# Float64 weights turned into float32 in two VectorE steps and a 16-bit ScalarE copy, in an attention and mixture-of-experts kernel

## The chip, the cores and the metric

One core of a Trainium2 chip runs the whole program. The metric is device time in microseconds (us) of one execution. The engines are TensorE (PE; its weight loads are PEld), VectorE (DVE), ScalarE (ACT), GpSimd (POOL) and SyncE (SP), whose queue issues the loads.

## The reference

The program is a chain of three layers over 1536 tokens of width 512.

```
attn: per head and block of 64: out = (q kT * decay) v + (q * powers) state ; state = decay * state + kT v
x  = attn_out reshaped to (1536, 512)
moe:  h = max(x @ w_in, 0) ; x = (h * h) @ w_out            # w_in (512, 2048), w_out (2048, 512)
moe2: logits = x @ w_gate ; each token goes to its best of 8 experts
      out = gate * sigmoid(x @ w_output_gate)[e] * (max(x @ w1[e], 0) @ w2[e])
```

`w_in` and `w_out` are scaled by a numpy float64, so they arrive as float64 (8 bytes a number, 16 MB in all). The kernel has to make float32 of them itself.

## The kernel before

**Attention.** The work is cut into 12 units `u` (two batches, six chunks of 128 tokens each). `emit_T` transposes q and k on PE, and ACT copies the result out (L268, L274). `emit_S` forms the scores, and DVE masks them into `sm` (L295). `emit_O` accumulates the output in the PSUM tile `po`, of which there is one; ACT rounds it into `xTh` (L317), and DVE forms the rest, `xTl` (L318). Only then can PE write `po` for the next unit. `emit_St` updates the state. POOL prepares decayed copies (`qd`, `kd`, `tmp`). In the body of unit u the order is: a weight load, the loads of q and k for u+4 and of v for u+3, `emit_T(u+2)`, `emit_S(u+1)`, `flush()`, `emit_O(u)`, `emit_St(u)`, `wconv`.

**Conversion.** 32 pieces of 128x512 float64 (512 KB each, alternately a block of `w_in` and of `w_out`) are loaded on SP's queue into four staging buffers `st` (`load_w`, L114 and L117). `conv_w` takes a piece's 32-bit halves: ACT scales the upper half into the float32 destination, which puts the exponent right and drops the sign (L131); DVE shifts the lower half right by 29 (L132), joins it with the destination shifted left by 3 (L135), and puts the sign back (L139). The first two are emitted by `wconv`; the last two wait in `rest_` for the next `flush()`. A staging buffer is free for piece i+4 after the last step of piece i. `WL` says how many pieces each unit loads, and `WA` how many it starts to convert.

**First expert layer.** Three chunks of 512 tokens, 16 steps `s` each. `mm1(s)` is 12 matmuls, `mm2(s-2)` 12 more. Every operand is split in a high and a low part (`wih`/`wil`, `woh`/`wol` by `split`, L356 on ACT and L357 on DVE; `gh`/`gl`, L386 and L387). `act1` takes the ReLU (`r`, L376 on ACT) and the square (`g`): in the first chunk on ACT (L379), in the others on DVE (L381). In the first chunk the 16 x 2 weight blocks are also converted and split: each step loads two pieces and converts two until all 32 are done. There is one buffer for `g` and one for `r`.

Each engine runs its instructions in the order of the program. The scheduler of the language adds the waits and moves nothing.

Of the kernel before, what the change touches and what calls it, by code (L numbers as in the profile page):

```python
# [11 lines left out]
BF16 = mybir.dt.bfloat16  # L12
I32 = mybir.dt.int32
I16 = mybir.dt.int16
U32 = mybir.dt.uint32
I64 = mybir.dt.int64
AF = mybir.ActivationFunctionType
ALU = mybir.AluOpType
# [6 lines left out]
def attn_moe_kernel(ctx, tc, q, k, v, lam, w_in, w_out, w_gate, w_ogate, w1, w2, out):  # L25
    nc = tc.nc
# [8 lines left out]
    NF = DFF // P  # L35
# [19 lines left out]
    nc.gpsimd.iota(io8, [[0, 1], [1, E]], base=0, channel_multiplier=0, allow_small_or_imprecise_dtypes=True)  # L55
    slots = const.tile([P, NG * P], I16, name="slots")
    nc.gpsimd.iota(slots, [[1, NG * P]], base=0, channel_multiplier=0, allow_small_or_imprecise_dtypes=True)
# [62 lines left out]
    def conv_w(i):  # L120
        f = i // 2
        t = staged.pop(i)
        if i % 2 == 0:
            dst = wiF[:, :, f * P:(f + 1) * P]
            sh = lambda a: a.rearrange("p (k f) -> p k f", k=KC)
        else:
            dst = woF[:, f, :]
            sh = lambda a: a
        w = t.bitcast(U32).rearrange("p (n w) -> p n w", w=2)
        lo, hi = w[:, :, 0], w[:, :, 1]  # L130
        nc.scalar.activation(out=dst, in_=sh(hi).bitcast(F32), func=AF.Copy, scale=2.0 ** -112)  # L131
        nc.vector.tensor_scalar(out=lo, in0=lo, scalar1=29, scalar2=None, op0=ALU.logical_shift_right)  # L132

        def shifted():
            nc.vector.scalar_tensor_tensor(out=sh(lo), in0=dst.bitcast(U32), scalar=3, in1=sh(lo),  # L135
                                           op0=ALU.logical_shift_left, op1=ALU.bitwise_or)

        def signed():
            nc.vector.scalar_tensor_tensor(out=dst.bitcast(U32), in0=sh(hi), scalar=0x80000000, in1=sh(lo),  # L139
                                           op0=ALU.bitwise_and, op1=ALU.bitwise_or)  # L140
        return shifted, signed


    sa = ExitStack()
# [10 lines left out]
    def cut(shape):  # L155
        n = 1
        for d_ in shape[1:]:
            n *= d_
        i = min(i for i in range(len(cas)) if cuts[i] + n <= KC * F2 // 2)
        o = cuts[i]  # L160
        cuts[i] = o + n
        v_ = cas[i][:, o:o + n]
        if len(shape) == 3:
            v_ = v_.rearrange("p (a b) -> p a b", b=shape[2])
        elif len(shape) == 4:
            v_ = v_.rearrange("p (a b c) -> p a b c", b=shape[2], c=shape[3])
        return v_
# [16 lines left out]
    def load_v(u):  # L184
        b, c = units[u]
        tv = ldv.tile([P, H, D], F32, tag="v", name="v")
        nc.sync.dma_start(out=tv, in_=v[b, :, c * P:(c + 1) * P, :].rearrange("h s d -> s h d"))
        qkv[u].append(tv)
# [56 lines left out]
    for b in range(B):  # L245
        t = cut([P, HP, P])
# [51 lines left out]
    def emit_O(u):  # L298
        b, c = units[u]
        vt = qkv[u][2]  # L300
        sm = sms.pop(u)
        qd = qds.pop(u, None)
        po = pO.tile([P, HP, P], F32, tag="po", name="po")

        if qd is not None:
            for hp in range(HP):
                for a in range(2):
                    sl = slice(a * D, (a + 1) * D)
                    nc.tensor.matmul(out=po[sl, hp, :], lhsT=state[b][:, hp, sl], rhs=qd[:, hp, :], start=hp == 0,  # L309
                                     stop=False)  # L310
        for hp in range(HP):
            for a in range(2):
                h = 2 * hp + a
                nc.tensor.matmul(out=po[a * D:(a + 1) * D, hp, :], lhsT=vt[:, h, :], rhs=sm[:, h, :],  # L314
                                 start=qd is None and hp == 0, stop=hp == HP - 1)
        t0 = b * S + c * P
        nc.scalar.copy(out=xTh[:, :, t0:t0 + P], in_=po)  # L317
        nc.vector.tensor_tensor(out=xTl[:, :, t0:t0 + P], in0=po, in1=xTh[:, :, t0:t0 + P].bitcast(F32),  # L318
                                op=ALU.subtract)

    def emit_tmp(u):
        b, c = units[u]
        if c in (0, NCH - 1):
            return
        tmps[u] = tmp = wa.tile([P, HP, D], F32, tag="tmp", name="tmp")
        for a in range(2):
            sl = slice(a * D, (a + 1) * D)
            nc.gpsimd.tensor_tensor(out=tmp[sl], in0=state[b][sl, :, a * D:(a + 1) * D], in1=lblk[sl], op=ALU.mult)

    def emit_St(u):  # L330
        b, c = units[u]
        vt = qkv.pop(u)[2]
        if c == NCH - 1:
            return
        kd = kds.pop(u)
        pt = pO.tile([P, HP, D], F32, tag="pt", name="pt", bufs=1)
        for hp in range(HP):
            for a in range(2):
                h = 2 * hp + a
                nc.tensor.matmul(out=pt[a * D:(a + 1) * D, hp, :], lhsT=kd[:, h, :], rhs=vt[:, h, :],  # L340
                                 start=True, stop=True)
        tmp = tmps.pop(u, None)
        for a in range(2):
            sl = slice(a * D, (a + 1) * D)
            if c == 0:
                nc.scalar.copy(out=state[b][sl, :, a * D:(a + 1) * D], in_=pt[sl])
                continue
            nc.vector.tensor_add(state[b][sl, :, a * D:(a + 1) * D], pt[sl], tmp[sl])
# [12 lines left out]
    def mm1(s):  # L361
        ch, f = divmod(s, NF)
        wih, wil = wis.pop(s)
        ps = pm.tile([P, NTC], F32, tag="ps", name="ps")
        tk = slice(ch * NTC, (ch + 1) * NTC)
        n = 0
        for kk in range(KC):
            for w_, x_ in ((wih, xTh), (wih, xTl), (wil, xTh)):
                nc.tensor.matmul(out=ps, lhsT=w_[:, kk, :], rhs=x_[:, kk, tk], start=n == 0, stop=n == 3 * KC - 1)  # L369
                n += 1  # L370
        hps[s] = ps

    def act1(s, mid=None):
        ps = hps.pop(s)
        r = gp[0].tile([P, NTC], F32, tag="r", name="r", bufs=1)
        nc.scalar.activation(out=r, in_=ps, func=AF.Relu)  # L376
        g = gp[0].tile([P, NTC], F32, tag="g", name="g", bufs=1)
        if s < NF:
            nc.scalar.activation(out=g, in_=r, func=AF.Square)  # L379
        else:  # L380
            nc.vector.tensor_mul(g, r, ps)  # L381
        if mid is not None:
            mid()
        gh = gp[0].tile([P, NTC], F32R, tag="gh", name="gh")
        gl = gp[0].tile([P, NTC], F32R, tag="gl", name="gl")
        nc.scalar.copy(out=gh, in_=g)  # L386
        nc.vector.tensor_tensor(out=gl, in0=g, in1=gh.bitcast(F32), op=ALU.subtract)  # L387
        gts[s] = gh, gl
# [18 lines left out]
    def wconv(n):  # L407
        m = min(n, NPC - wc[0])
        wc[0] += m
        return [conv_w(wc[0] - m + i) for i in range(m)]  # L410

    rest_ = []

    def flush():
        for step in range(2):
            for r_ in rest_:
                r_[step]()
        rest_.clear()

    WA = (0,0,0,0,1,1,1,1,1,1,2,0)  # L420
    WL = (0,0,1,1,1,1,1,1,1,1,1,1)
    load_v(0)
    load_qk(2)
    load_v(1)
# [8 lines left out]
    for u in range(NU):  # L433

        first = u < 2
        if first:
            emit_O(u)
            emit_St(u)
        emit_tmp(u)
        wload(WL[u])  # L440
        if u + 4 < NU:
            load_qk(u + 4)
        if u + 3 < NU:
            load_v(u + 3)
        if u == 0:
            emit_S(u + 1)
        if first:
            decays(u)
        if u + 2 < NU:
            emit_T(u + 2)  # L450
        if u == NU - 3:

            sqk.close()
            sp[0] = sab.enter_context(tc.tile_pool(name="sp", bufs=2, side="right", reuse_waits="tile"))
        if u == NU - 2:
            split_in(0)
        if 0 < u < NU - 1:
            emit_S(u + 1)
        if u == NU - 2:
            split_in(1)  # L460
        flush()
        if u == NU - 1:
            mm1(0)
        if not first:
            emit_O(u)
            emit_St(u)
        rest_ += wconv(WA[u])
    mm1(1)
    wload(2)
    sa.close()  # L470
# [62 lines left out]
    def route_max(ch):  # L533
        nc.tensor.transpose(p_lg, lgT, ident)
        m8 = const.tile([P, NTT, 8], F32, tag="m8", name="m8")
        i8 = const.tile([P, NTT, 8], U32, tag="i8", name="i8")
        lg = const.tile([P, NTT, 2 * E], F32, tag="lg", name="lg")
# [515 lines left out]
    for e in range(E):  # L1053
        for f in range(NF2):
            s = e * NF2 + f
# [65 lines left out]
```

## Time and profile before

| | us |
|---|---|
| median of 3 runs (561.15 to 562.47) | 562.06 |
| the profiled execution | 560.67 |
| its span, first to last instruction | 558.9 |
| PE busy | 536.4 (96%) |
| DVE busy | 361.6 (65%) |
| ACT busy | 304.1 (54%) |
| granted TensorE clock | 0.995 |

The shares are means over the span. Attention fills the first 68 us, the first chunk of the first expert layer about 68 to 156 us, its other two chunks follow up to about 340 us, and the routed experts take the rest. PE's busy time has gaps in the attention and hardly any in the expert layer.

### The profile page before, as it was taken

Reading aid. Unit: us, or ns where it says so; the run is one execution under the profiler, and the core shown is the slowest. Engines: PE = TensorE matmul, PEld = TensorE weight load, DVE = VectorE, ACT = ScalarE, POOL = GpSimd, SP = SyncE. Lnnn points to the kernel's source line nnn. Section 1 sums busy time; section 2 is a strip of 40 time slices with the busy share of each in tenths; the row PEclk is TensorE's granted clock in tenths of the full one; section 3 lists DMA queues with packets and bytes.
Section 4 is the critical chain, followed back from the end, with each engine's and each line's share of the span. In section 5 each row is a group of like instructions: output and inputs, shape, how many; then the busy total and the mean of one; then the engine's idle time right before and its main releaser. Section 6 shows DMA issues by size and latency. Waiting matters only on the chain.

```text
span 558.9 us, 9785 instructions
## 1 busy us (share of the span) xinstructions
PE 536.4 (96%) x3601; PEld 458.1 (82%) x3601; DVE 361.6 (65%) x728; ACT 304.1 (54%) x580; POOL 149.2 (27%) x149
## 2 busy tenths in 40 slices
PE   7898899999999999999999999999999999999993
PEld 6787788878878888887888888889888889888982
DVE  4789988989455674546676446948264948875610
ACT  4765487776653444445444434447264857884610
POOL 4688000000021232422124241450313142240101
PEclk9999999999999999999999999999999999999998
DMA  8999445568200000000000003999638667830000
GB/s 198 227 245 246 152 153 204 173 205 302 95 1 1 20 34 24 1 0 1 19 20 19 20 0 116 391 228 350 207 114 287 205 206 260 280 133 20 9 24 23
DMA packets 75045, 72.88 MB, mean 130 GB/s; under 512 B 30181, under 2 KB 61029, under 8 KB 74976
## 3 DMA queue, kind: packets, MB, share of 16 engines
q1 hardware_dynamic: 70624, 62.96, 35.9%
q0 software_dynamic: 4064, 8.91, 5.2%
q8 instruction: 43, 0.70, 0.6%
q14 instruction: 26, 0.21, 0.1%
q10 hardware_dynamic: 288, 0.10, 0.1%
HBM read 65.84 MB, written 9.29 MB: 134 GB/s over the span
## 4 chain that ended last, share of the span: by engine, by line
PE 62%; issue 22%; DVE 6%; POOL 4%; DMA 2%; ACT 2%; SPq 1%; POOLq 0%; another core or an unknown queue 0%; ACTq 0%; DVEq 0%
PE acc L497 23%; PE ps L369 22%; PE ph L936 5%; PE ea L958 5%; POOL out_dram L968 3%; POOL xg L895 2%; DMA k<-in_k_dram 2%; PE po L314 1%; PE po L309 1%; PE px L710 1%; PE ps L293 1%; DVE sm L295 1%; DMA out_dram<-y,sidx 1%; DVE xTl L318 1%; PE pl L528 1%
## 5 line engine op out<-in xcount | busy, mean ns | idle before, releaser
L357 POOL TENSOR_TENSOR wol<-woF,woh 128x512 fp32r<-128x512 f32 x32 | 41.3, 1292 | 222.4 <-ACT woh L356 222.4
L387 DVE TENSOR_TENSOR gl<-g,gh 128x512 fp32r<-128x512 f32 x48 | 52.6, 1097 | 65.6 <-ACT gh L386 65.6
L936 PE MATMUL ph<-xh,xTh 128*128 128x192 f32 (+2 forms) x256 | 76.9, 301 | 0.7 <-DVE xl L921 0.4
L369 PE MATMUL ps<-xTh,wih 128*128 128x512 f32 x192 | 76.5, 398 | 0.0
L497 PE MATMUL acc<-gh,woh 128*128 128x512 f32 x192 | 75.0, 390 | 0.5 <-DVE x1T L509 0.5
L497 PE MATMUL acc<-gl,woh 128*128 128x512 f32 x192 | 75.4, 393 | 0.0
L497 PE MATMUL acc<-gh,wol 128*128 128x512 f32 x192 | 74.8, 390 | 0.0
L369 PE MATMUL ps<-xTl,wih 128*128 128x512 f32 x192 | 74.8, 390 | 0.0
L369 PE MATMUL ps<-xTh,wil 128*128 128x512 f32 x192 | 74.8, 389 | 0.0
L936 PE MATMUL ph<-xh,xTl 128*128 128x192 f32 (+2 forms) x256 | 74.7, 292 | 0.0
L951 DVE SCALAR_TENSOR_TENSOR hl<-ph,hh 128x384 fp32r<-128x384 f32 (+1 forms) x64 | 34.2, 534 | 62.1 <-ACT hh L950 49.0
L936 PE MATMUL ph<-xl,xTh 128*128 128x192 f32 (+2 forms) x256 | 74.3, 292 | 0.0
L356 ACT CAST woh<-woF 128x512 fp32r<-128x512 f32 x48 | 29.5, 615 | 57.9 <-PE acc L497 55.7
L936 PEld LDWEIGHTS ph<-xh,xTh 128*128 128x128 f32 x256 | 48.6, 190 | 6.9 <-DVE hl L951 4.3
L950 ACT ACTIVATE hh<-ph 128x384 fp32r<-128x384 f32 (+1 forms) x64 | 30.8, 482 | 37.4 <-PE ph L936 33.3
L936 PEld LDWEIGHTS ph<-xl,xTh 128*128 128x128 f32 x256 | 48.6, 190 | 0.8
L936 PEld LDWEIGHTS ph<-xh,xTl 128*128 128x128 f32 x256 | 48.8, 190 | 0.2 <-DVE xTl L811 0.2
L376 ACT ACTIVATE r<-ps 128x512 f32<-128x512 f32 x48 | 28.5, 594 | 35.5 <-PE ps L369 35.4
L895 POOL DMA_INDIRECT xg<-x1d,gidx x21 | 24.5, 1168 | 83.9 <-PE pt L915 62.3
L968 POOL DMA_INDIRECT out_dram<-y,sidx x23 | 23.7, 1029 | 76.6 <-ACT y L967 73.6
L811 DVE TENSOR_TENSOR xTl<-w1r,xTh 128x512 fp32r<-128x512 f32 x64 | 43.6, 685 | 0.1
L497 PEld LDWEIGHTS acc<-gl,woh 128*128 128x128 f32 x192 | 36.0, 188 | 9.0 <-DVE gl L387 1.6
(189 smaller groups left out, 1154.0 us busy)
## 6 DMA issues: line engine op xcount, KB each, us to landing
w1r<-in_moe_w_dram SPq DMA_DIRECT2D x32, 512.0 KB
w2r<-in_moe_w_dram SPq DMA_DIRECT2D x32, 512.0 KB
st<-in_moe_w_in_dram SPq DMA_DIRECT2D x16, 512.0 KB
st<-in_moe_w_out_dram SPq DMA_DIRECT2D x16, 512.0 KB
q<-in_q_dram SPq DMA_DIRECT2D x24, 128.0 KB
k<-in_k_dram SPq DMA_DIRECT2D x12, 256.0 KB
v<-in_v_dram SPq DMA_DIRECT2D x12, 256.0 KB
x1d<-xr SPq DMA_DIRECT2D x12, 256.0 KB
```

The lines of the kernel that those rows point to most:

```text
L356: nc.scalar.copy(out=hi, in_=src)
L357: eng.tensor_tensor(out=lo, in0=src, in1=hi.bitcast(F32), op=ALU.subtract)
L369: nc.tensor.matmul(out=ps, lhsT=w_[:, kk, :], rhs=x_[:, kk, tk], start=n == 0, stop=n == 3 * KC - 1)
L376: nc.scalar.activation(out=r, in_=ps, func=AF.Relu)
L387: nc.vector.tensor_tensor(out=gl, in0=g, in1=gh.bitcast(F32), op=ALU.subtract)
L497: nc.tensor.matmul(out=acc[ch][cb], lhsT=w_[:, cs], rhs=x_, start=f == 0 and i == 0, stop=f == NF - 1 and i == 2)
L811: eng.tensor_tensor(out=lo, in0=src, in1=hi.bitcast(F32), op=ALU.subtract)
L895: nc.gpsimd.indirect_dma_start(out=out_, out_offset=None, in_=x1d[:, :], in_offset=bass.IndirectOffsetOnAxis(ap=ix, axis=0), bounds_check= ...
L936: nc.tensor.matmul(out=ps[:, 0:N], lhsT=w_[:, kk, :], rhs=x_[:, kk, 0:N], start=n == 0, stop=n == 3 * KC - 1)
L950: nc.scalar.activation(out=hh[:, f, ts_], in_=ps[:, ts_], func=AF.Relu)
L951: nc.vector.scalar_tensor_tensor(out=hl[:, f, ts_], in0=ps[:, ts_], scalar=0.0, in1=hh[:, f, ts_].bitcast(F32), op0=ALU.max, op1=ALU.subtract)
L968: nc.gpsimd.indirect_dma_start(out=outs[j][:, :], out_offset=bass.IndirectOffsetOnAxis(ap=sidx[:, j, e:e + 1], axis=0), in_=ys[j], in_offs ...
```

## The change

A piece's lowest three mantissa bits, which lie at the top of the lower half, are first brought next to the upper half's bits: ACT copies 16 bits of the lower half over the low 16 bits of the upper half (after the scaled copy has read it). One DVE instruction then shifts the upper half right by 13, with its sign, and masks it to the sign and three bits. A second one joins that with the destination shifted left by 3. So DVE runs two instructions for each piece instead of three, and ACT two instead of one; and DVE's first one now comes after ACT's copy. `flush()` has one step, and runs once more behind the attention's last unit. The square of the first chunk is taken on DVE, as in the other chunks. By `WL` the attention loads pieces from unit 3 on instead of 2, nine instead of ten; by `WA` it starts to convert them in unit 5 instead of 4, seven instead of eight.

```diff
+        h = t.bitcast(U16).rearrange("p (n w) -> p n w", w=4)
         nc.scalar.activation(out=dst, in_=sh(hi).bitcast(F32), func=AF.Copy, scale=2.0 ** -112)
-        nc.vector.tensor_scalar(out=lo, in0=lo, scalar1=29, scalar2=None, op0=ALU.logical_shift_right)
-
-        def shifted():
-            nc.vector.scalar_tensor_tensor(out=sh(lo), in0=dst.bitcast(U32), scalar=3, in1=sh(lo),
+
+        nc.scalar.copy(out=h[:, :, 2], in_=h[:, :, 1])
+        nc.vector.tensor_scalar(out=lo.bitcast(I32), in0=hi.bitcast(I32), scalar1=13, scalar2=-0x7ffffff9,
+                                op0=ALU.arith_shift_right, op1=ALU.bitwise_and)
+
+        def join():
+            nc.vector.scalar_tensor_tensor(out=dst.bitcast(U32), in0=dst.bitcast(U32), scalar=3, in1=sh(lo),
                                            op0=ALU.logical_shift_left, op1=ALU.bitwise_or)
-
-        def signed():
-            nc.vector.scalar_tensor_tensor(out=dst.bitcast(U32), in0=sh(hi), scalar=0x80000000, in1=sh(lo),
-                                           op0=ALU.bitwise_and, op1=ALU.bitwise_or)
-        return shifted, signed
+        return join
...
-        if s < NF:
-            nc.scalar.activation(out=g, in_=r, func=AF.Square)
-        else:
-            nc.vector.tensor_mul(g, r, ps)
+        nc.vector.tensor_mul(g, r, ps)
...
-        for step in range(2):
-            for r_ in rest_:
-                r_[step]()
+        for r_ in rest_:
+            r_()
...
-    WA = (0,0,0,0,1,1,1,1,1,1,2,0)
-    WL = (0,0,1,1,1,1,1,1,1,1,1,1)
+    WA = (0,0,0,0,0,1,1,1,1,1,1,1)
+    WL = (0,0,0,1,1,1,1,1,1,1,1,1)
...
         rest_ += wconv(WA[u])
+    flush()
     mm1(1)
```

In the changed kernel's line numbers the loads stand one higher, `conv_w` one to four higher, the rest up to the square one higher, and what follows the square two lower. SP's queue in units 1 to 3, before: `st` is a staging buffer.

```order
L179 DMA q<-in_q_dram 64x4x128 x2
L181 DMA k<-in_k_dram 128x8x64
L187 DMA v<-in_v_dram 128x8x64
L114 DMA st<-in_moe_w_in_dram 128x4x128
L179 DMA q<-in_q_dram 64x4x128 x2
L181 DMA k<-in_k_dram 128x8x64
L187 DMA v<-in_v_dram 128x8x64
L117 DMA st<-in_moe_w_out_dram 128x512
```

The same place of the change:

```order
L180 DMA q<-in_q_dram 64x4x128 x2
L182 DMA k<-in_k_dram 128x8x64
L188 DMA v<-in_v_dram 128x8x64
L180 DMA q<-in_q_dram 64x4x128 x2
L182 DMA k<-in_k_dram 128x8x64
L188 DMA v<-in_v_dram 128x8x64
L115 DMA st<-in_moe_w_in_dram 128x4x128
```

The first piece has moved behind the q, k and v of one more unit, and every later piece with it. So five pieces instead of six stand ahead of the last k.

VectorE at the end of the attention, from the scores of the last unit to the low part of step 2's weights, before:

```order
L295 TENSOR_TENSOR sm<-ps,ca_142 128x4x128 x2
L357 TENSOR_TENSOR wil<-wiF,wih 128x512
L135 SCALAR_TENSOR_TENSOR st<-woF,st 128x512
L139 SCALAR_TENSOR_TENSOR woF<-st 128x512
L318 TENSOR_TENSOR xTl<-po,xTh 128x4x128
L132 TENSOR_SCALAR st<-st 128x512 x2
L135 SCALAR_TENSOR_TENSOR st<-wiF,st 128x512
L135 SCALAR_TENSOR_TENSOR st<-woF,st 128x512
L139 SCALAR_TENSOR_TENSOR wiF<-st 128x4x128
L139 SCALAR_TENSOR_TENSOR woF<-st 128x512
L318 TENSOR_TENSOR xTl<-po,xTh 128x4x128
L357 TENSOR_TENSOR wil<-wiF,wih 128x512
```

And in the change:

```order
L296 TENSOR_TENSOR sm<-ps,ca_142 128x4x128 x2
L358 TENSOR_TENSOR wil<-wiF,wih 128x512
L140 SCALAR_TENSOR_TENSOR wiF<-wiF,st 128x4x128
L319 TENSOR_TENSOR xTl<-po,xTh 128x4x128
L136 TENSOR_SCALAR st<-st 128x512
L140 SCALAR_TENSOR_TENSOR woF<-woF,st 128x512
L319 TENSOR_TENSOR xTl<-po,xTh 128x4x128
L136 TENSOR_SCALAR st<-st 128x512
L140 SCALAR_TENSOR_TENSOR wiF<-wiF,st 128x4x128
L379 TENSOR_TENSOR g<-r,ps 128x512
L358 TENSOR_TENSOR wil<-wiF,wih 128x512
```

One instruction instead of two stands ahead of the first `xTl` here, and two instead of six between the two. But a shift, a join and the square now stand between the last `xTl` and `wil`, where nothing stood.

ScalarE in one step of the first chunk, from the ReLU to the last conversion, before:

```order
L376 ACTIVATE r<-ps 128x512
L379 ACTIVATE g<-r 128x512
L356 CAST woh<-woF 128x512
L356 CAST wih<-wiF 128x512
L386 CAST gh<-g 128x512
L131 ACTIVATE wiF<-st 128x4x128
L131 ACTIVATE woF<-st 128x512
```

And in the change:

```order
L377 ACTIVATE r<-ps 128x512
L357 CAST woh<-woF 128x512
L357 CAST wih<-wiF 128x512
L384 CAST gh<-g 128x512
L133 ACTIVATE woF<-st 128x512
L135 COPY st<-st 128x512
L133 ACTIVATE wiF<-st 128x4x128
L135 COPY st<-st 128x512
```

The square is gone, and each scaled copy is followed by a 16-bit copy; the pieces of a step are now `w_out` first, then `w_in`, since an odd number is converted ahead.

## Rows read from the trace of the kernel before

**Rows 1.** The page: rate of transfers in 40 slices, and packets.
```profile
GB/s 198 227 245 246 152 153 204 173 205 302 95 1 1 20 34 24 1 0 1 19 20 19 20 0 116 391 228 350 207 114 287 205 206 260 280 133 20 9 24 23
DMA packets 75045, 72.88 MB, mean 130 GB/s; under 512 B 30181, under 2 KB 61029, under 8 KB 74976
```

**Rows 2.** Busy time of three stretches: each engine, clock, DMA share, GB/s.
```profile
34.00:55.00 21.00, 17.20 (x316) 15.37 (x316) 20.48 (x31) 13.21 (x28) 18.20 (x18) 1.00 0.97 247
55.00:69.00 14.00, 12.17 (x167) 10.58 (x164) 13.74 (x26) 6.71 (x14) 2.13 (x2) 1.00 0.55 167
101.00:142.00 41.00, 41.00 (x179) 32.67 (x178) 35.58 (x66) 28.76 (x51) 0.00 (x0) 1.00 0.71 246
```

**Rows 3.** TensorE in order of time, 53 to 72 us: start, duration, idle time before.
```profile
54.78 0.46 PE L263 MATMUL psT<-ident,k 64*128 64x64 f32 x8 [0.91 <-DMA k<-in_k_dram]
...
60.69 1.09 PE L309 MATMUL po<-qd,ca 128*64 128x128 f32 x16 [1.05 <-DVE xTl L318]
...
66.38 1.09 PE L309 MATMUL po<-qd,ca 128*64 128x128 f32 x16 [0.78 <-DVE xTl L318]
...
68.28 0.50 PE L369 MATMUL ps<-xTh,wih 128*128 128x512 f32 x1
...
71.49 0.19 PEld L369 LDWEIGHTS ps<-xTh,wil 128*128 128x128 f32 x1 [0.15 <-DVE wil L357]
```

**Rows 4.** SyncE's queue, issues of q: first and last of two stretches.
```profile
5.53 2.35 SPq L179 DMA_DIRECT2D q<-in_q_dram  x2
...
16.75 1.69 SPq L179 DMA_DIRECT2D q<-in_q_dram  x2
...
21.25 1.26 SPq L179 DMA_DIRECT2D q<-in_q_dram  x2
...
48.65 1.26 SPq L179 DMA_DIRECT2D q<-in_q_dram  x2
```

**Rows 5.** The chain that ended last: the last k, and the first chunk.
```profile
50.03 4.71 DMA k<-in_k_dram
...
101.26 2.79 PE acc L497 x12
104.04 2.72 PE ps L369 x12
...
142.94 2.27 PE ps L369 x10
```

**Rows 6.** VectorE in order of time, 59 to 66 us.
```profile
59.25 0.69 DVE L139 SCALAR_TENSOR_TENSOR wiF<-st 128x512 uint32<-128x512 uint32 x1
59.86 0.68 DVE L318 TENSOR_TENSOR xTl<-po,xTh 128x512 fp32r<-128x512 f32 x1
...
64.94 0.69 DVE L139 SCALAR_TENSOR_TENSOR woF<-st 128x512 uint32<-128x512 uint32 x1
65.55 0.68 DVE L318 TENSOR_TENSOR xTl<-po,xTh 128x512 fp32r<-128x512 f32 x1
```

**Rows 7.** Groups by form on VectorE and ScalarE: busy us, mean ns, idle before.
```profile
L132 DVE TENSOR_SCALAR st<-st 128x512 uint32<-128x512 uint32 x32 | 12.6, 430 | 0.2
...
L381 DVE TENSOR_TENSOR g<-r,ps 128x512 f32<-128x512 f32 x32 | 21.9, 684 | 11.7 <-ACT r L376 11.7
...
L131 ACT ACTIVATE wiF<-st 128x512 f32<-128x512 f32 x16 | 11.0, 686 | 1.8 <-DMA st<-in_moe_w_in_dram 1.4
```

**Rows 8.** Waits in 99 to 146 us: total, times, longest.
```profile
ACT g L379 <- DVE gl L387: 8.8, 9, 2.9
```

**Rows 9.** ScalarE and VectorE in order of time at the first chunk's start.
```profile
68.39 0.59 ACT L317 CAST xTh<-po 128x512 fp32r<-128x512 f32 x1 [3.98 <-PE po L314]
...
69.57 0.63 ACT L379 ACTIVATE g<-r 128x512 f32<-128x512 f32 x1
70.11 0.60 ACT L356 CAST wih<-wiF 128x512 fp32r<-128x512 f32 x1
...
70.74 0.69 DVE L357 TENSOR_TENSOR wil<-wiF,wih 128x512 fp32r<-128x512 f32 x1 [0.82 <-ACT wih L356]
```

More of the change, by code (lines that the diff above doesn't have):

```diff
@@ L14 @@
 I16 = mybir.dt.int16
+U16 = mybir.dt.uint16
 U32 = mybir.dt.uint32
```

## The prediction

> **What bounds the kernel now.** I read the busy time by stretches first, then TensorE's own idle time, and then what ended it. From 101 to 142 us PE is busy for 41.00 of 41 us [rows 2], and the expert layers behind that look alike: what is gained ahead of them is kept, what is lost ahead of them is paid. The gaps are in the attention. From 34 to 69 us PE is busy for 29.4 of 35 us, while DVE is busy for 34.2 of them and the DMA engines, up to 55 us, at 0.97 of their time [rows 2]. So two things are full at once there, and the order of time tells which of them ends PE's waits. At 54.78 us PE waits 0.91 us for the last k [rows 3], which was issued at 50.03 and took 4.71 us to come [rows 5]. That is a queue in front of the DMA engines, and the chain runs through it. Behind it the chain is DVE: at 60.69 and 66.38 us PE waits 1.05 and 0.78 us for `xTl` [rows 3], that is for the single `po` to be free. Each time `xTl` stands right behind conversion steps [rows 6]. The first chunk shows a third thing. Its blocks take 2.72 us where nothing is missing [rows 5], but from 101.26 to the start of the `mm1` block at 142.94 us there are 15 blocks in 41.68 us, where 15 x 2.72 is 40.80: 0.88 us are lost. DVE is busy for 35.58 of 41 us there and its idle time is forced: ACT's square waits for `gl` [rows 8], since there is one `g`, and the split behind it on DVE waits for ACT in turn.
>
> **The loads.** One piece fewer stands ahead of the last k on SP's queue. SP issues q, k and v of three units in 11.22 us without pieces (5.53 to 16.75), 3.74 each, and of five units with one piece each in 27.40 us (21.25 to 48.65), 5.48 each [rows 4]. The piece costs the difference, 1.74 us. The bounds: by bytes at the stretch's 247 GB/s [rows 2], 512 KB take 2.12 us; at the highest rate of any slice, 391 GB/s [rows 1], 1.34 us. I take 1.75, since it is measured on this queue: **-1.75**.
>
> The Trainium skill (DMA: Bandwidth & Descriptors, Specifications) says that transfers under 512 bytes don't reach the line rate, and gives a ceiling of 435 GB/s. 30,181 of the packets here are under 512 bytes [rows 1]; the rows of k and v are 256 bytes, those of the pieces 1 and 4 KB. By its ceiling a piece would take 1.2 us, an estimate, and the sum below would be 3.0 us and not 3.56. That the piece costs less than its bytes at the mean rate agrees; by how much is what the queue's rows say.
>
> Does the rest keep pace? DVE loses one join of the two in every unit, at 0.69 us and above [rows 6], and the whole first conversion, so it no longer fills its time. The first conversion's loads and steps keep their distance of two units.
>
> **The end of the attention.** Ahead of each of the two late `xTl` one instruction of 0.69 us goes [rows 6], and DVE comes to them earlier, because it lags less. With one join, the first `xTl` needs only `xTh` (0.59 us on ACT [rows 9]) and itself (0.68), 1.3 us behind the end of `emit_O`; on PE `emit_St` and `emit_S` lie behind that for about 1.6 us. The second has all of `mm1(0)` as its cover, 2.72 us, against masks, a split and a join on DVE that start earlier by the first wait. So both waits go: **-1.83**. The bound is what one join of 0.69 us at each would give, 1.38, less a little for the new wait of the shift on ACT's 16-bit copy: 1.2.
>
> **The 16-bit copy.** The trace has none. From below, ACT's cast of as many elements takes 0.60 us [rows 9]; the scaled copy, which also reads every second word, 0.686 [rows 7]. I take 0.69, since it has the same stride. Twice that, 1.4 us, would be writing at half the rate. In the attention it stands where ACT waits for PE (3.98 us before the last `xTh` [rows 9]). In the first chunk a step of ACT then holds four instructions of 0.60 and four of 0.69 us, 5.2 us, against 5.44 for two blocks of PE, and successive ones overlap a little (0.63 us of square, 0.54 from its start to the next [rows 9]). It fits, narrowly. If that cover is gone, each 0.1 us of the copy costs 0.2 us a step.
>
> **The new shift** has one tensor operand as the old one, 0.43 us [rows 7]. If two operations made it as slow as a join, 0.69, DVE would still have room. In order, it holds the masks and splits behind it until ACT's copy is done; ACT's copy comes right behind `xTh`, and the shift behind two state additions, so I price it at nothing, except here:
>
> **The start of the first chunk** pays. Before, ACT ran `xTh`, `r`, `g`, `wih`, and DVE's `wil` started 2.35 us after `xTh` did (68.39 to 70.74 [rows 9]); PE, which needs it for its third matmul of `mm1(2)`, waited 0.15 us [rows 3]. Now the last piece's two copies come between `xTh` and `r`, and DVE has shift, join and square ahead of `wil`. In start-to-start times: `xTh` 0.5, two copies 1.2, the shift 0.4, the join 0.6, `g` 0.6, which makes 3.3 us. `wil` starts 0.95 us later, and PE's wait grows by about as much: **+0.9**. The bounds are 0.5, if joins and copies overlap better, and 1.2, with full durations. What is late next is `gl` of step 1, by the same amount; it has about 1 us to spare before `mm2(1)`.
>
> **The first chunk** then runs as DVE and PE let it. DVE's step was two shifts, two splits, four joins and `gl`; now two joins are gone and the square (0.684 [rows 7]) is added: 2 x 0.43 + 6 x 0.69 = 5.0 us, and by start-to-start times 4.4. More important, `g` no longer crosses from `gl` to ACT and back. Both engines are under 5.44, so the 0.88 us come back: **-0.88**; from below, 0.4, if ACT is late now and then. There is one step more with a conversion, and the first experts' loads follow one step later (about 5 us), some 200 us before they are used: nothing.
>
> **The sum.** -1.75 - 1.83 + 0.9 - 0.88 = -3.56. The profiled execution took 560.67 us, 558.9 of them in its span; it would take 557.1. The median of the runs is 562.06, so I forecast **558.5 us**. With all bounds at their good end the gain is 2.12 + 1.83 + 0.88 - 0.5 = 4.3, at their bad end 1.34 + 1.2 + 0.4 - 1.2 = 1.7: 557.7 to 560.3.
>
> **Rivals.**
> - *The loads don't hurry the attention.* DVE has no idle time there, so the k may be late by chance of the same rhythm, or the queue may lose the time elsewhere, as q, k and v of later units wait for buffers that POOL frees (busy for 18.2 of 21 us [rows 2]). Against it: PE does wait for k, with the whole queue filled. Then 1.75 fall away: 560.3 us. Chance 0.13.
> - *The start and the handshake eat it.* DVE's shift waits for ACT in each unit and step, ACT for DVE's `g` before `gh`. If the start of the first chunk costs 3.5 us more instead of 0.9, as three waits of a join and a copy in a row would, it is 561 to 562.5 us: no change. For it: ACT has 0.25 us to spare in a step by full durations. Against it: the waits of a step don't close a circle. Chance 0.09.
> - *ACT becomes the bound of the first chunk.* With a copy of 1.4 us its step is 4 x 0.54 + 2 x 0.6 + 2 x 1.3 = 6.0 us, 0.55 over PE's, in 12 steps 6.6, less about 1 us of slack, and the 0.88 are not won: 562.06 - 2.7 + 5.6 = 565 us. It begins at about 1.05 us for a copy and makes the kernel slower from about 1.3. For it, nothing but that a 16-bit write isn't in the trace; against it, that ACT's other forms lie between 0.59 and 0.69. Chance 0.08.
>
> **The numbers.** The forecast with its bounds has 0.70. A change under 0.2%, 1.1 us, is about what cannot be told from none. Faster is the forecast and the first rival, 0.83; same is the second, 0.09; slower the third, 0.08. For 8 in 10 I take the forecast and the first rival with 0.7 us at the low end for the unknown and 0.6 at the high end: 557.0 to 560.9.
>
> **What would show it.** In the changed profile the last k should land near 53 us, and no wait for `xTl` of over 0.3 us should stand behind it; `mm1(1)` should start near 64.8 us instead of 68.28. PE's third matmul of `mm1(2)` should wait about 1 us for `wil`. From 100 to 140 us the blocks should be 2.72 us each, with ACT busy for about 5 us a step. The 16-bit copy should take 0.6 to 0.75 us, the shift 0.43. I am wrong if the copy takes over 1 us, if k lands at 54.7 us again, or if PE waits for `gl` or for `r` in the first steps.

## The result and the profile after

The changed kernel takes 565.12 us (median of 8 runs, 564.14 to 566.88) against 561.61 us (8 runs) before, on the same chip: a ratio of 1.0073, 95% interval 1.0056 to 1.0091. It is slower by 3.5 us where 3.6 us less were forecast, and it lies outside the range. The third rival came about: ScalarE becomes the bound of the first chunk. The profiled execution took 566.84 us, the second longest of the eight and 1.7 over their median; 565.1 of them lie in its span, 6.2 over the one of before. So the split by stages below is that of a dear execution.

Busy time of the stretches of [rows 2], in the changed kernel (TensorE, weight loads, VectorE, ScalarE, GpSimd, clock, DMA share, GB/s):

```profile
34.00:55.00 21.00, 17.98 (x332) 16.54 (x332) 17.77 (x30) 18.73 (x34) 17.48 (x18) 0.96 0.99 253
55.00:69.00 14.00, 13.38 (x157) 11.49 (x156) 9.26 (x16) 8.98 (x15) 1.42 (x1) 0.93 0.45 133
...
101.00:142.00 41.00, 40.64 (x171) 31.29 (x170) 31.64 (x57) 40.56 (x58) 0.00 (x0) 1.00 0.59 183
```

In the attention VectorE falls from 20.48 to 17.77 of 21 us, as the change means it to. From 101 to 142 us ScalarE goes from 28.76 to 40.56 of 41 us: it has no idle time left. TensorE still shows 40.64, but it starts 171 matmuls there instead of 179. A busy time close to full is no proof of full speed; the count beside it is what tells.

ScalarE in order of time, one step of the first chunk (start, duration):

```profile
100.05 0.71 ACT L377 ACTIVATE r<-ps 128x512 f32<-128x512 f32 x1
100.64 0.62 ACT L357 CAST woh<-woF 128x512 fp32r<-128x512 f32 x1
101.14 0.64 ACT L357 CAST wih<-wiF 128x512 fp32r<-128x512 f32 x1
101.66 0.64 ACT L384 CAST gh<-g 128x512 fp32r<-128x512 f32 x1
102.18 0.69 ACT L133 ACTIVATE woF<-st 128x512 f32<-128x512 f32 x1
102.90 1.39 ACT L135 COPY st<-st 128x512 uint16<-128x512 uint16 x1
104.01 0.72 ACT L133 ACTIVATE wiF<-st 128x512 f32<-128x512 f32 x1
104.76 1.38 ACT L135 COPY st<-st 128x512 uint16<-128x512 uint16 x1
105.86 0.70 ACT L377 ACTIVATE r<-ps 128x512 f32<-128x512 f32 x1
```

No row waits. From `r` to the next `r` there are 5.81 us, and two blocks of TensorE are 5.44. The two copies hold 1.11 and 1.10 of it from start to start, the scaled copies ahead of them 0.72 and 0.75.

The groups of the copy, the shift and the square in the first 156 us (busy us, mean ns, idle before), beside [rows 7]:

```profile
L135 ACT COPY st<-st 128x512 uint16<-128x512 uint16 x32 | 44.1, 1379 | 1.0
L136 DVE TENSOR_SCALAR st<-st 128x512 int32<-128x512 int32 x32 | 14.2, 443 | 20.0 <-ACT st L135 19.9
L379 DVE TENSOR_TENSOR g<-r,ps 128x512 f32<-128x512 f32 x16 | 11.0, 687 | 1.1 <-ACT r L377 1.0
```

The shift (0.443 us) and the square (0.687) cost what was said; the copy takes 1.379 us instead of 0.69. The waits from 69 to 157 us (total, times, longest) show what has taken the place of the wait in [rows 8]:

```profile
DVE st L136 <- ACT st L135: 18.9, 15, 1.4
PEld ps L370 <- DVE wil L358: 5.6, 12, 0.6
PE ps L370 <- DVE g L379: 2.4, 2, 1.6
```

VectorE no longer holds ScalarE up; it waits for ScalarE's copy in every step, and TensorE's weight loads, twelve times, for the split `wil` behind it.

TensorE in order of time, from the last k to `mm1(2)`, beside [rows 3]:

```profile
53.53 0.69 PE L264 MATMUL psT<-ident,k 64*128 64x64 f32 x8 [1.64 <-DMA k<-in_k_dram]
54.01 2.02 PE L294 MATMUL ps<-ca 64*128 64x128 f32 x16
55.97 1.52 PE L310 MATMUL po<-qd,ca 128*64 128x128 f32 x16
...
59.86 1.09 PE L310 MATMUL po<-qd,ca 128*64 128x128 f32 x16
...
65.40 1.09 PE L310 MATMUL po<-qd,ca 128*64 128x128 f32 x16 [0.62 <-DVE xTl L319]
...
67.30 0.50 PE L370 MATMUL ps<-xTh,wih 128*128 128x512 f32 x1
...
71.91 0.47 PE L370 MATMUL ps<-xTh,wih 128*128 128x512 f32 x1 [1.58 <-DVE g L379]
...
74.82 0.39 PE L495 MATMUL acc<-gh,woh 128*128 128x512 f32 x1
```

The last k lands 1.25 us earlier, the first wait for `xTl` is gone, and `mm1(1)` starts at 67.30 instead of 68.28. Then `mm1(2)` waits 1.58 us, and for `g`, not for `wil`. Comparing marks in the two traces splits the 6.2 us: up to `mm1(1)` -0.98; to the first matmul of `mm2(0)` (73.89 before, 74.82 after) +1.91; to the last `gl` of the chunk (160.24 before, 165.96 after) +4.79; behind it +0.5.

The chain of waits now leads through the copy. By engine (ScalarE had 2% before), and two of its links:

```profile
PE 66%; ACT 14%; issue 10%; DVE 4%; DMA 2%; POOL 1%; POOLq 0%; SPq 0%; another core or an unknown queue 0%; ACTq 0%
```

```profile
102.90 1.39 ACT st L135
...
104.76 1.38 ACT st L135
```

### The profile page after: what moved, and what is told of

Same layout as the page of the kernel before. It is cut to its first block, busy times and chain, and to the rows that moved or that the text cites. A ratio compares the mean times of both kernels' runs of the same rounds, so it can differ in the third digit from the quotient of the medians.

```text
span 565.1 us, 9816 instructions
## 1 busy us (share of the span) xinstructions
PE 542.5 (96%) x3601; PEld 460.5 (81%) x3601; DVE 351.8 (62%) x712; ACT 332.8 (59%) x596; POOL 146.7 (26%) x149
## 4 chain that ended last, share of the span: by engine, by line
PE 66%; ACT 14%; issue 10%; DVE 4%; DMA 2%; POOL 1%; POOLq 0%; SPq 0%; another core or an unknown queue 0%; ACTq 0%
PE acc L495 18%; PE ps L370 16%; PE ph L934 13%; PE ea L956 11%; ACT st L135 6%; ACT gh L384 1%; PE ps L294 1%; ACT woF L133 1%; ACT wiF L133 1%; PE po L310 1%; ACT ca L269 1%; PE po L315 1%; DMA k<-in_k_dram 1%; PE px L708 1%; PE pt L913 1%
## 5 line engine op out<-in xcount | busy, mean ns | idle before, releaser
L370 PE MATMUL ps<-xTh,wil 128*128 128x512 f32 x192 | 76.2, 397 | 0.7 <-DVE wil L358 0.2
L377 ACT ACTIVATE r<-ps 128x512 f32<-128x512 f32 x48 | 30.2, 630 | 37.0 <-PE ps L370 37.0
L370 PEld LDWEIGHTS ps<-xTh,wil 128*128 128x128 f32 x192 | 36.0, 188 | 13.0 <-DVE wil L358 5.6
L370 PEld LDWEIGHTS ps<-xTh,wih 128*128 128x128 f32 x192 | 36.1, 188 | 11.1 <-ACT wih L357 2.6
L135 ACT COPY st<-st 128x512 uint16<-128x512 uint16 x32 | 44.1, 1379 | 1.0
```

The source lines that it names most:

```text
L135: nc.scalar.copy(out=h[:, :, 2], in_=h[:, :, 1])
```

## The experiments

**Theory A:** the copy costs twice what was assumed, and this alone makes ScalarE the bound of the first chunk; the other terms hold. **Theory B:** the new handshakes (shift for copy, `gh` for `g`) make the steps longer, whatever the copy takes. With them goes the question why the copy takes so long. Each ratio is to runs of the kernel before on the same chip.

**The copy at the price of a word.** ScalarE copies a whole 32-bit word at the same place, over the lower half, and VectorE's shift still comes after it; the lowest three bits of the mantissa are then other bits.

```
-        nc.scalar.copy(out=h[:, :, 2], in_=h[:, :, 1])
+        nc.scalar.copy(out=lo.bitcast(F32), in_=hi.bitcast(F32))
```

> The changed kernel with its 16-bit copy replaced by a copy of 32-bit words of the same pieces, at the same place and with the same waits (the three lowest mantissa bits of the weights are then other bits). Theory A, the price of the 16-bit copy (1.38 us in the changed profile) makes ScalarE the bound of the first chunk: the copy should take about 0.69 us, ScalarE's step fall from 5.80 to about 4.5 us of starts, TensorE's from 5.80 to 5.44, and the time to 557.5 to 559.5 us, under before's 561.6. Theory B, the waits of VectorE's shift and square on ScalarE cost the time whatever a copy takes: 562 us or more.

Measured: 557.96 us, ratio 0.9934 [0.9910, 0.9958], span 555.5 where the sum of the prediction gave 555.3. The copy's group, TensorE's marks, and links of the chain:

```profile
L135 ACT COPY st<-st 128x512 f32<-128x512 f32 x32 | 20.9, 654 | 0.0
```

```profile
52.63 0.46 PE L264 MATMUL psT<-ident,k 64*128 64x64 f32 x8 [0.63 <-DMA k<-in_k_dram]
...
57.82 1.09 PE L310 MATMUL po<-qd,ca 128*64 128x128 f32 x16 [0.32 <-DVE xTl L319]
...
64.68 0.50 PE L370 MATMUL ps<-xTh,wih 128*128 128x512 f32 x1
...
68.44 0.47 PE L370 MATMUL ps<-xTh,wih 128*128 128x512 f32 x1 [0.72 <-DVE g L379]
...
71.34 0.39 PE L495 MATMUL acc<-gh,woh 128*128 128x512 f32 x1
```

```profile
101.43 2.72 PE ps L370 x12
104.15 2.72 PE acc L495 x12
```

With a copy of 0.654 us the sum lands, and with it `mm1(1)` at 64.68 (forecast 64.8) and the blocks of 2.72. The handshakes are all still there, but the shift waits for ScalarE for only 2.4 us in all in the first chunk, against 18.9, so B falls.

**What in the copy is dear.** A kernel of copies alone (all else of the computation is left out), 128x512 each, four of each form, on tiles of 8-byte groups.

```
+        nc.scalar.copy(out=dense(ts["readstr_o"]), in_=low(ts["readstr_i"]))
+        nc.scalar.copy(out=high(ts["writestr_o"]), in_=dense(ts["writestr_i"]))
```

> A probe that leaves out the whole computation and runs copies of 128 x 512 elements, four of each form: 16 bits in place with a step of 8 bytes as in the change (1.38 us is known), the same into another tile, dense to dense, step to dense, dense to step, the same bits as bfloat16, and 32-bit words with a step and dense; then the form of the change on VectorE and on GpSimd. If the 16-bit write with a step is what costs, dense to step is about 1.38 us and step to dense about 0.6. If the read is, the reverse. If the integer type is, the bfloat16 form is about 0.65 and dense to dense of 16-bit integers stays high. If reading and writing the same tile is, the form into another tile is about 0.65.

The groups (busy us, mean ns):

```profile
L55 ACT COPY inplace<-inplace 128x512 uint16<-128x512 uint16 x4 | 5.6, 1409 | 0.0
...
L57 ACT COPY dense_o<-dense_i 128x512 uint16<-128x512 uint16 x4 | 3.1, 780 | 0.0
L58 ACT COPY readstr_o<-readstr_i 128x512 uint16<-128x512 uint16 x4 | 2.9, 720 | 0.0
L59 ACT COPY writestr_o<-writestr_i 128x512 uint16<-128x512 uint16 x4 | 5.4, 1358 | 0.0
L60 ACT COPY bfl<-bfl 128x512 bf16<-128x512 bf16 x4 | 5.4, 1359 | 0.0
L61 ACT COPY word<-word 128x512 f32<-128x512 f32 x4 | 2.9, 728 | 0.0
```

Reading 16 bits every 8 bytes is cheap (0.720), writing them there is dear (1.358); another type (bf16, 1.359) or another tile (1.450) changes nothing, and a 32-bit word at the same step is cheap in both directions (0.728). So it is the write of half words with a step, on this engine: VectorE's first copy of the same form took 0.67 us. Why ScalarE takes so long for it no run shows.

**The old three steps with the square on VectorE and the later loads.** (The conversion of before, rest of the change.)

```
-        nc.scalar.copy(out=h[:, :, 2], in_=h[:, :, 1])
...
+        nc.vector.tensor_scalar(out=lo, in0=lo, scalar1=29, scalar2=None, op0=ALU.logical_shift_right)
...
+        return shifted, signed
```

> The three-step conversion of before with the rest of the change (loads and conversions one unit later, one flush more, square of the first chunk on VectorE). Theory A: no 16-bit copy, so the first chunk isn't bound by ScalarE; VectorE's step is 2 x 0.38 + 8 x 0.60 = 5.6 us of starts, about before's 5.57; the attention gains from the loads: 559.5 to 561.5 us. Theory B (moving the square to VectorE makes the start and the steps wait): 563 us or more.

Measured: 560.15 us, 0.9970 [0.9956, 0.9985]. VectorE is busy for 41.00 of 41 us from 101 to 142 us, and the blocks still take 2.72; waits for `xTl` of 0.94 and 0.76 us stay.

**The later loads alone** (the kernel before, with the new `WA`, `WL` and the last `flush`).

```
+    WA = (0,0,0,0,0,1,1,1,1,1,1,1)
+    WL = (0,0,0,1,1,1,1,1,1,1,1,1)
```

> Before with the new numbers of loads and conversions per unit alone (and the flush that they need). If the loads are worth what the forecast said, the last k lands about 1.75 us earlier; VectorE still has two joins in each unit, so part of it may stay at VectorE: 559.5 to 561 us. If VectorE alone set the attention's length: 561 to 562 us, no change.

Measured: 560.20 us, 0.9972 [0.9957, 0.9987]. TensorE no longer waits for the last k; `mm1(1)` starts at 66.59 instead of 68.28, and the waits for `xTl` are 0.65, 0.94 and 0.78 us. The loads, with the conversions one unit later, are worth about 1.4 us by themselves. They also bring a cost at the start of the first chunk: a piece now stands between the last unit's output and `mm1(2)`, whose weight loads wait for both splits behind it:

```profile
69.63 0.19 PEld L369 LDWEIGHTS ps<-xTh,wih 128*128 128x128 f32 x1 [0.44 <-ACT wih L356]
...
70.53 0.19 PEld L369 LDWEIGHTS ps<-xTh,wil 128*128 128x128 f32 x1 [0.60 <-DVE wil L357]
```

This kernel and the one above differ only in the engine that takes the square in the first chunk, and their times agree. The marks show why. From `mm1(1)` to `mm2(0)` there are 6.34 us (66.59 to 72.93) with ScalarE's square and 6.91 (67.42 to 74.33) with VectorE's, against 5.61 before; from there to the last `gl` of the chunk 86.19 (to 159.12) and 85.47 (to 159.80), against 86.35 before. What the square's move wins in the steps it loses, but for 0.15 us, at the start.

**The new conversion alone**, with ScalarE's square and the old loads.

```
+        if s < NF:
+            nc.scalar.activation(out=g, in_=r, func=AF.Square)
+        else:
+            nc.vector.tensor_mul(g, r, ps)
```

> Before with the new conversion alone (square on ScalarE, loads and conversions per unit as before). Theory A: ScalarE's step is 5.80 plus a square of 0.54, 6.3 us of starts, 0.77 over before's 5.57 in 12 steps, 9 us, and the attention has one copy more: 568 to 573 us. If moving the square was a loss by itself, this is faster than the change: under 565.

Measured: 571.34 us, 1.0194 [1.0170, 1.0219]. From 101 to 142 us ScalarE is busy for 40.40 us and TensorE for 38.12; a step takes 6.48 us. One more instruction on ScalarE costs 0.67 us a step: ScalarE is the bound, as A has it.

**Half of the pieces.** Only those of `w_in` get the 16-bit copy, those of `w_out` the old three steps.

```
+        if i % 2 == 0:
...
+            nc.scalar.copy(out=h[:, :, 2], in_=h[:, :, 1])
```

> The change with only the w_in pieces converted with the 16-bit copy, the w_out pieces in the three steps of before. Theory A: ScalarE's step is 4 x 0.53 + 2 x 0.70 + 1.10 = 4.6 us, VectorE's 2 x 0.38 + 7 x 0.60 = 5.0 us, both under TensorE's 5.44: the first chunk runs without loss, 558 to 560 us. Theory B: 562 us or more.

Measured: 559.36 us, 0.9965 [0.9949, 0.9981]. One copy of 1.38 us a step fits: from 85 to 150 us all blocks but two (2.96 and 2.75) take 2.72 us.

**The first chunk's copies on GpSimd.**

```
-        nc.scalar.copy(out=h[:, :, 2], in_=h[:, :, 1])
+        (nc.scalar.copy if i < 7 else nc.gpsimd.tensor_copy)(out=h[:, :, 2], in_=h[:, :, 1])
```

> The change with the first chunk's 16-bit copies on GpSimd, which is idle there, and the attention's seven left on ScalarE. Theory A: ScalarE's step falls to 4 x 0.53 + 2 x 0.60 = 3.3 us, the first chunk runs at 5.44 a step if GpSimd's copy takes under about 2.2 us, and the time is 559 to 561.5 us; if GpSimd's copies hold up VectorE's instructions of two SBUF operands, 561.5 to 564. Theory B, the waits of VectorE on another engine's copy: 563 us or more.

Measured: 566.80 us, 1.0118 [1.0103, 1.0134], over both ranges of theory A. It lies in the range of B, but not by B's waits: from 69 to 155 us VectorE's shift waits for GpSimd's copy for 1.3 us in all. GpSimd's copy takes 1.632 us; GpSimd, two copies in one row, and VectorE in order of time beside it:

```profile
99.66 3.13 POOL L135 COPY st<-st 128x512 uint16<-128x512 uint16 x2 [2.97 <-ACT woF L133]
...
99.39 0.67 DVE L140 SCALAR_TENSOR_TENSOR woF<-woF,st 128x512 uint32<-128x512 uint32 x1
99.99 1.58 DVE L140 SCALAR_TENSOR_TENSOR wiF<-wiF,st 128x512 uint32<-128x512 uint32 x1
101.49 1.59 DVE L385 TENSOR_TENSOR gl<-g,gh 128x512 fp32r<-128x512 f32 x1
```

The same join takes 0.67 or 1.58 us, and VectorE is busy for 41.00 of 41 us from 101 to 142 us. The Trainium skill (SBUF — State Buffer, "SBUF: two separate sides") says that a VectorE operation with two SBUF inputs and a GpSimd operation that reads SBUF exclude each other for a whole instruction. The trace agrees: beside GpSimd's copies a join and `gl` are each stretched by 0.9 us in every step. The traces of before and of the change held the sign already, in `gl` from the end of the first chunk on, where GpSimd makes the splits `wol`: 1.37 and 1.36 us instead of 0.69.

**A wide write.** ScalarE reads the half word and writes a 32-bit word; VectorE keeps both joins and loses the shift.

```
+        nc.scalar.activation(out=lo, in_=h[:, :, 1], func=AF.Copy, scale=2.0 ** -13, bias=-4095.5 / 8192)
```

> The change with another second ScalarE instruction: it reads the same 16 bits with a step, scales them by 2 to the -13 and writes the three bits as a 32-bit word into the lower half, so VectorE needs no shift and runs the two joins of before. By the copy forms, a read of 16 bits with a step and a wide write should take about 0.7 us. Theory A (the 16-bit write with a step is the cost): ScalarE's step is 4 x 0.53 + 4 x 0.60 = 4.5 us, VectorE's 8 x 0.60 = 4.8 us, both under 5.44: the first chunk without loss; the attention as in the run with the loads alone: 558.5 to 560 us. If the read of 16 bits with a step costs too, 563 us or more.

Measured: 559.75 us, 0.9968 [0.9950, 0.9986]. The group shows a half word read and a word written at 0.675 us:

```profile
L134 ACT ACTIVATE st<-st 128x512 uint32<-128x512 uint16 x32 | 21.6, 675 | 0.0
```

The joins remain, and so do waits for `xTl`, 1.05 and 0.44 us.

**The joins behind `xTl`.** The same, with `flush()` behind `emit_O` and `emit_St` instead of ahead of them; and the old three steps with the same move.

```
-        flush()
         if u == NU - 1:
             mm1(0)
         if not first:
             emit_O(u)
             emit_St(u)
+        flush()
```

> The same with the joins of each unit behind that unit's output instead of ahead of it on VectorE, so that the low part of the output doesn't wait for them. If the two late waits of TensorE for it (0.94 and 0.78 us in the run with the loads alone) stem from the joins ahead of it, they go: 1 to 1.7 us less than the run with the wide write, 557 to 558.5 us. If the work is only moved to the next unit's masks, the same as that run.

> The three-step conversion of before with the rest of the change (560.2 us) and the joins behind each unit's output. If the late waits go as above: 558.5 to 559.5 us; if they are only moved, 560 us.

Measured: 560.20 us, 0.9979 [0.9967, 0.9991], and 562.40 us, 1.0012 [0.9994, 1.0030]. The gain came in neither: the first can't be told from the run with the wide write (559.75), which is the second of the two outcomes expected, and the other is slower than both that were expected. The late waits for `xTl` are gone in both, and come back behind them. TensorE in the first of the two:

```profile
65.52 0.50 PE L371 MATMUL ps<-xTh,wih 128*128 128x512 f32 x1
...
70.34 0.47 PE L371 MATMUL ps<-xTh,wih 128*128 128x512 f32 x1 [1.78 <-DVE g L380]
```

In the second `mm1(2)` waits 2.35 us for `g`, and ahead of that TensorE waits for the last masks and then runs its scores slowly (granted clock 0.65 from 58 to 61 us):

```profile
58.29 2.51 PE L293 MATMUL ps<-ca,ca 64*128 64x128 f32 x16 [1.55 <-DVE sm L295]
```

What VectorE doesn't do ahead of `xTl` it does ahead of the masks and of the square of step 0.

**New conversion where ScalarE has room, old one where not.** Pieces 0 to 5 (the attention's, but for its seventh) the new way, the other 26 the old way; in the first of two kernels the square of step 0 is on ScalarE again.

```
-        if i % 2 == 0:
+        if i < 6:
...
+        if s == 0:
+            nc.scalar.activation(out=g, in_=r, func=AF.Square)
```

> The six pieces of the attention are converted the new way, the other 26 the old way (three steps, no 16-bit copy), and step 0 alone has its square on ScalarE again; the rest as in the changed kernel. Theory (the copy's price counts only where ScalarE has no idle time, and the first wait of mm1(2) is for the tile that the square of step 0 frees): mm1(1) starts near 64.8 us, mm1(2) waits 0.2 to 0.4 us as it did before, and the blocks of the first chunk take 2.72 us: median 557.5 to 558.7. Rival (the copies cost as much in the attention too): mm1(1) not before 66 us and a median of 559.5 or more. Second rival (the start of mm1(2) is held by the split wil and not by the square): mm1(2) waits 0.8 us or more in spite of the square on ScalarE, 558.5 to 559.3.

> As the run beside it, but with every square on VectorE. If the square of step 0 holds mm1(2), its wait is 0.8 to 1.2 us here, by 0.6 or more longer than beside it, and the median is about 0.7 us above it: 558.2 to 559.4. If wil holds it, both kernels wait alike and their times agree.

Measured: 558.56 us, 0.9945 [0.9926, 0.9964], and 558.64 us, 0.9943 [0.9921, 0.9965]. TensorE at the start of `mm1(2)`, in the first kernel and in the second:

```profile
71.54 0.50 PE L380 MATMUL ps<-xTh,wih 128*128 128x512 f32 x1
...
72.44 0.50 PE L380 MATMUL ps<-xTh,wil 128*128 128x512 f32 x1 [0.17 <-DVE wil L368]
```

```profile
64.85 0.50 PE L380 MATMUL ps<-xTh,wih 128*128 128x512 f32 x1
...
68.87 0.47 PE L380 MATMUL ps<-xTh,wih 128*128 128x512 f32 x1 [1.01 <-DVE g L389]
```

TensorE waits 0.17 us for `wil` with the square on ScalarE and 1.01 us for `g` with it on VectorE: there the square, which frees the `ps` of step 0, holds `mm1(2)`. It isn't the whole delay. From `mm1(1)` to `mm2(0)` there are 6.36 us (68.51 to 74.87) and 6.93 (64.85 to 71.78), so the square's move costs 0.57 us here, as in the pair above; the rest of the delay over the 5.61 of before is there with ScalarE's square too. The expected 0.7 us between the medians doesn't show. In the first kernel's profiled execution TensorE waited 2.28 us for a late q in the attention, and `mm1(1)` started at 68.51 and not near 64.8; its single runs span 557.4 to 561.5 us, which hides a difference of this size. Both beat the kernel before by 3 us and the changed one by 6.5 (565.12 to 558.6).

## Why the prediction was wrong, point by point

- **The 16-bit copy is the step that failed.** "I take 0.69, since it has the same stride" was the term: measured 1.379 us, at the upper bound of 1.4 that stood beside it. The choice was made by the nearest rows, which all write words; the write of half words with a step isn't among them, and that is what costs. The rule of the Trainium skill that would have borne on it (SBUF — State Buffer, the note on SBUF's cachelines under "Door 1: The DMA port swizzle") asks for two accesses to a line of 16 bytes, which a step of 8 bytes gives for reading and writing alike. Here reading at that step takes 0.720 us and writing 1.358, so the measurement decides.
- **The first chunk, "-0.88".** +4.79 in the profiled execution. The rival's sum for a copy of 1.4 us gave a step of 6.0 us and 565 us in all; measured are 5.81 us and 565.12. The sign came from this alone: from `mm2(0)` to the last `gl` of the chunk there are 160.24 - 73.89 = 86.35 us before, 156.81 - 71.34 = 85.47 with the word copy, which is -0.88, and 165.96 - 74.82 = 91.14 in the changed kernel. Of the 5.67 us between the last two, the steady steps make up most: `r` starts at 77.03 and, eleven steps on, at 140.68, 5.79 us each, which is 0.35 over TensorE's 5.44 and 3.8 in all. Another 1.4 lie in the first step, where `r` starts 2.21 us behind `mm2(0)` against 0.78 with the word copy.
- **The loads and the waits for `xTl`, -1.75 and -1.83.** With the word copy `mm1(1)` starts 3.60 us earlier against 3.58 forecast, though divided otherwise: k lands 2.15 us earlier, and 0.32 us of waiting stays. Its whole span is 3.4 us shorter, which lies between the 3.56 by the rows and the estimate of 3.0 by the ceiling of the Trainium skill (DMA: Bandwidth & Descriptors, Specifications) and tells neither from the other. With half of the copies and with six of them `mm1(1)` stands at 64.74 and 64.85, so where no transfer comes late the dear copy doesn't hurt in the attention, as the prediction had it. In the other kernel with six of them a late q put it at 68.51. The changed kernel's profiled execution won only 0.98 of this: its k took 5.85 us to come, the stretch behind it ran at a lower clock, and a wait of 0.62 us stayed. Why k and that q came late in those executions, and whether the copies have a part in it, is open.
- **The start of the first chunk, "+0.9" by `wil`.** With the word copy it is +1.05, with the real one +1.91. The size was about right, the wait that was named only a part: `mm1(2)` waits already at its first matmul, for `g`. That `ps` of step 0 is now freed by the square on VectorE, behind shift and join of the last piece, stood in the code and was missed. From `mm1(1)` to `mm2(0)` the runs show three parts: the last piece ahead of the splits costs 0.73 us with the old steps (loads alone, 6.34 against 5.61), the square on VectorE another 0.57 (6.91 and 6.93), and the 16-bit copy for that last piece another 0.55 (half of the pieces: 64.74 to 72.22, 7.48).
- **The shift, "0.43"**, and the square were right (0.443, 0.687).
- **The rivals.** Loads that don't hurry the attention: refuted, the loads alone bring 1.4 us. The handshakes: refuted by the word copy. ScalarE as the bound: right, with its mechanism and its price. That its 565 us agree with the median is in part luck: it put the first chunk at +5.6 us, the start at +0.9 and the attention at -3.58, where the profiled execution shows +4.79, +1.91 and -0.98, and it counted from 562.06, where eight runs have 561.61. 0.08 was too little for a price with one bound at twice the other, on an engine with 0.25 us to spare.

## What to carry to other kernels

Before work moves to an engine with 5% to spare, measure the one operation whose form isn't in the trace: element size and step of the write count, not only the number of elements. If an operation is dear on an engine, use it only in the stretches where that engine waits anyway, and keep the old form elsewhere. When an operation that reads a PSUM tile last changes engines, follow who waits for that tile.

## What the runs showed of the hardware

- ScalarE writes 512 half words per partition, 8 bytes apart, in 1.36 to 1.45 us, reads them in 0.72, and writes 32-bit words at the same step in 0.65 to 0.73. In the kernel of copies VectorE's first copy of the same form, in place, took 0.67 us with GpSimd idle, and its last 1.75 beside GpSimd's copies, which took 1.61 in the mean.
- In the changed kernel's profiled execution TensorE's granted clock fell behind the wait for k. Two stretches of 3 us (columns as above):

```profile
51.00:54.00 3.00, 1.17 (x18) 0.89 (x18) 2.76 (x5) 2.12 (x3) 2.29 (x3) 0.91 0.97 251
54.00:57.00 3.00, 3.00 (x34) 2.78 (x32) 0.93 (x2) 2.12 (x5) 0.00 (x0) 0.52 0.89 261
```

TensorE was busy for 1.17 of 3 us, then ran mostly at the lower level of 1.2 GHz: sixteen score matmuls took 2.02 us instead of the 1.11 of an earlier unit, and the `po` behind them 1.52 instead of 1.09. By these two rows that made the late k about 1.3 us dearer, an estimate. With the word copy, where k was waited for 0.63 us, the clock from 54 to 57 us was 1.00. Behind the late q, a wait of 2.28 us, it was 0.71 in the same 3 us. Of the changed kernel's eight runs the two longest (566.84 and 566.88 us) have a mean clock of 0.988, the others (564.14 to 565.88) 0.991 to 0.995.
